# A longer planned slack behind crossbar turns for TensorE's work, in attention followed by a gated feed-forward layer

## The chip, the cores and the metric

The kernel runs on one core of a Trainium2 chip. The metric is the device time of one execution in microseconds (us). A core has five engines that run programs of their own and meet at semaphores: TensorE (PE in the profile, with its weight loads as PEld), VectorE (DVE), ScalarE (ACT), GpSimd (POOL) and SyncE (SP). SP does no arithmetic here; it issues transfers. The kernel before takes 334.26 us, the median of five runs that lie between 333.06 and 335.65 us.

## The reference

Causal attention by blocks of 64 tokens, and then one feed-forward layer whose activation is a swish with a slope of its own for each hidden unit:

```python
# B, H, S, D = 8, 8, 576, 64;  d_model 512, d_ff 2048
scores = scale * np.matmul(q, k.transpose(0, 1, 3, 2))
scores = np.where(block_i >= block_j, scores, -1e9)      # blocks of 64
attn = softmax(scores)
attn_out = np.matmul(attn, v)
x = attn_out.transpose(0, 2, 1, 3).reshape(B * S, H * D)  # 4608 x 512
h = x @ w_in
g = h * (1.0 / (1.0 + np.exp(-beta * h)))
out = g @ w_out
```

## The kernel before

**Two streams of work on one PE.** Attention goes by batch and, within a batch, by pair of heads: a unit `u` is one pair of one batch, four units to a batch, 32 in all. The feed-forward layer goes by chunks of 512 rows of x, nine of them, `r` = 0 to 8. A chunk needs the batches `b0` to `b1` that its rows lie in; for chunks 3 to 7 the last batch is the one with the chunk's own number, and chunk 8 needs no batch beyond 7. The two streams are laid into each other on PE: attention runs about one and a half batches ahead of the chunks that need it.

**Attention.** Q and K have to stand with the head dimension on the partitions. For batches 0 and 1 PE turns them (L634) and DVE copies them out of PSUM. From batch 2 on (`QB = 2`) the turn is a transfer: POOL casts both to bf16 (L665, `QKn`), and SP issues a transfer that turns two units at once through the DMA engines' crossbar into `QKT` (L672, the group of semaphores called `d_T`). There are twelve of these. PE then makes the scores (L708, with the array divided into two halves of 64 rows, the mode `row`): three visits for two units, each an operation of the plan. ACT takes the exponentials into `E` (L724), DVE clears the masked corners (L730, L732), PE multiplies with the values (L764, which bring a column of ones along for the row sums), and DVE divides by the sums (L776, L783) into `xq`.

**From attention to the layer.** The layer needs x turned once more, as `xT`. For batches 0 to 2 PE turns it (L813). From batch 3 on (`XB = 3`) it is again a crossbar transfer from SP, one for each unit (L800, semaphores `d_TX...`), two where the ring buffer of `xT` wraps.

**The layer.** For each chunk there are sixteen up-projections (`fh`, L1000: four matmuls of 128 x 512 into one PSUM bank), each followed by a tanh on ACT (L1010) and a combination on DVE (L1014) that gives sixteen tiles of `gT`. The down-projection (`prod`, L921) is done in chunks 1 to 8 by seven products of half size instead of eight, each in two operations of eight matmuls, with sums of `gT` and of the weights prepared by DVE (L885). So a chunk has 14 such operations of down-projection. In chunk 0 it is the plain one (L1036). Results go out from ACT's queue.

**The order is planned.** No engine's order is written out by hand. `Plan.op` records an operation with an expected duration, a priority (lower goes first), what it depends on and what tiles it needs; `Plan.schedule` then plays the program through, and at each moment gives a free engine the eligible operation of lowest priority. An operation is eligible at its planned `ready` (the planned end of its last dependency, plus `SEM` = 70 ns) plus its own `rest`, and on PE plus `SLACK` = 120 ns:

```python
slack = self.SLACK if e == "PE" else 0.0
if o.ready + o.rest + slack > now + 1e-9:
    heapq.heappush(events, o.ready + o.rest + slack)
    continue
```

The planned end of a transfer is when it has passed its ring plus `LAND` = 2600 ns (L141); its time in the ring is the `xfer` that it was given, 3200 ns for a turn of Q and K and 1100 ns for one of x, if nothing else is in the ring. What comes out of the plan is the order of each engine's instructions, the buffers and banks that tiles are given, and the semaphore waits that follow from them. The planned times themselves are not in the program: on the chip each engine runs its list as fast as the semaphores let it.

`rest` is 0 unless it is set. L827 to L829 set it to 300 ns for operations of PE that depend directly on one of SP or POOL (loads, casts and the turns of Q and K), if they have none yet. This loop stands ahead of the place where the chunks are recorded (L989 on), so the up-projections, which come later, keep 0.

PE's priorities: scores and other work of a unit of batch `b` >= 2 have 994 + 100 * (b - 1.5) + 4.9 * c and a fraction (`pr`), up-projections 1000 + 100 r + j, and the products of the down-projection 1000 + 100 r + 16 for the first two operations, and for the others 103 and up, which is among the next chunk's up-projections. PE also has fillers without use, until 50 us of the plan (L515).

Of the kernel before, what the change touches and what calls it, by code (L numbers as in the profile page):

```python
# [359 lines left out]
def bass_blockwise_causal_attn__then__act_swish_beta_kernel(  # L360
# [10 lines left out]
    with es:  # L371
# [4 lines left out]
        QB, XB, CAST = 2, 3, "POOL"  # L376
# [44 lines left out]
        P = Plan()  # L421
# [6 lines left out]
        def mm(n):  # L428
            return max(n / 2.4 + 3, 55.0)

        def act_t(n, ptr=0):
            return 0.833 * n + 93 + 93 * ptr

        def dve_t(n):
            return (n + 125) / 0.96

        LAG = 1.5
        def pr(u):
            b, c = divmod(u, NPAIR)
            return u if b < 1 else 10 * u if b < 2 else 994 + 100 * (b - LAG) + 4.9 * c  # L440
# [14 lines left out]
        def mk(fn):  # L455
            return lambda g, e: fn(g)
# [13 lines left out]
        for i in range(NQ):  # L470
# [5 lines left out]
            o = P.op("POOL", 200, mk(lambda g, i=i: g.memset(Vn[i][:, 4, :, 64:66], 0.0)), prio=-5)  # L476
# [40 lines left out]
        for i in range(NFILL):  # L517
# [11 lines left out]
            o = P.op("PE", n, ff, deps=[c2, c4], tiles=[tf], lat=n, mode="full", prio=1e6 + i)  # L529
# [6 lines left out]
        for b in range(B):  # L536
# [4 lines left out]
            for h0, h1, e, tt in PARTS[b]:  # L541

                vs = []
                for i in tt:
# [10 lines left out]
                    if e == "SP":  # L555
                        o = P.op("SP", 300 + 550 * n, fv, tiles=[ts], xfer=1400 * n,
                                 prio=3.5 + 0.1 * (h0 > 0) if b == 0 else 4 * b + (3.5 if b < 2 else 0.5),
                                 dma=["d_V", h0, 1])
                    else:
                        o = P.op("POOL", 150 + 1450 * n, fv, tiles=[t], xfer=1400 * n, prio=-30 if b == 0 else 4 * b + (3.5 if b < 2 else 0.5), dma=["d_VP", h0, 1])  # L560
# [9 lines left out]
                for g0 in range(h0, h1, 2):  # L570
                    g1 = g0 + 2

                    def fw(g, e, ts=ts, t=t, g0=g0, g1=g1, n=n):
                        return g.tensor_copy(Vn[t.slot][:, 0:n, g0:g1, 0:64], Vs[ts.slot][:, 0:n, g0:g1, :])  # L574

                    o = P.op("POOL", 60 + 60 * n * (g1 - g0), fw, deps=[*vs, *ones, *vzero], tiles=[ts, t],
                             prio=4 * b + 0.5 - (38.5 - 4.6 * (h0 > 0)) * (b < 1))
# [23 lines left out]
        for u in range(NU):  # L601
# [8 lines left out]
            if b < QB:  # L610

                turned = []
                for w, (nm, src) in enumerate((("Q", q), ("K", k))):
# [7 lines left out]
                    o = ld[nm, u] = P.op("SP", 420, fl, tiles=[ts], xfer=1170, prio=u, dma=["d_S", 0, 1])  # L621
                    o.pkt = 80.0

                    def fn(g, e, ts=ts, tn=tn, p=p, w=w):
# [4 lines left out]
                    o = P.op("POOL" if onp else "DVE", 850 if onp else 750, fn, deps=[o], tiles=[ts, tn],  # L629
                             prio=-40 + 3 * u if onp else -1)  # L630

                    def ft(g, e, tn=tn, pt=pt, p=p, w=w):
                        for i in range(6):
# [4 lines left out]
                    o = P.op("PE", 6 * 43, ft, deps=[o, c4], tiles=[tn, pt, tt_], lat=6 * 43 + 170, mode="full",  # L638
                             prio=pr(u))
# [8 lines left out]
            elif p == 0:  # L648

                for w, (nm, src) in enumerate((("Q", q), ("K", k))):  # L650
                    ts = P.tile("S4")

                    def fl(g, e, ts=ts, src=src, b=b, c=c):
# [3 lines left out]
                    o = P.op("SP", QKI, fl, deps=[o for t in early6 for o in t.users] if b == QB else [],  # L657
                             tiles=[ts], xfer=QKX, prio=u, dma=["d_S4", 0, 1])
# [20 lines left out]
            if b not in JOIN or p == 0:  # L679
# [4 lines left out]
                for grp in visits:  # L684
# [3 lines left out]
                    def fq(g, e, pst=pst, grp=grp, tqk=tqk, b=b):  # L688
                        keep = {}
                        for (uu, g0), ps in zip(grp, pst):  # L690
# [4 lines left out]
                            for t, q0, q1, off in blocks:  # L695
# [18 lines left out]
                    o = P.op("PE", n, fq, deps=cps, tiles=list({id(x): x for x in pst}.values()) + [tqk] + [tes[uu] for uu in sorted({uu for uu, _ in grp})] * (b > 0),  # L714
                             lat=n + 200, mode="row", prio=pr(u) + .2 if len(grp) == 4 else pr(u + 1) + .1 if grp[0][0] > u else
                             pr(u) + .1 + .1 * (grp[0][1] >= 2))
# [3 lines left out]
            for g0 in range(4):  # L720
                o, ps = qk[g0]
# [105 lines left out]
        for o in P.ops:  # L827
            if o.idx > 40 and o.engs == ("PE",) and not o.fill and any(d.engs == ("SP",) or d.engs == ("POOL",) for d in o.deps) and not o.rest:
                o.rest = 300.0  # L829
        win[0].deps += [ld["K", 0]]  # L830
        for o in ld["VP", 0, 4]:
            o.deps += [ld["K", 2]]
# [156 lines left out]
        for r in range(NRC):  # L989
            row = RC * r  # L990
            b0, b1 = row // S, (row + RC - 1) // S
            xd = [xt[4 * b + c] for b in range(b0, b1 + 1) for c in range(4)]
            tg = P.tile("gT")
            gs, hs = [], []
            for j in range(NJ):
                ph, tt = P.tile("P1"), P.tile("th")

                def fh(g, e, ph=ph, j=j, row=row):
                    for c in range(4):
                        z = g.matmul(PS[:, ph.slot, :], w_in[:, c, 128 * j:128 * j + 128], xT[:, c, row % RX:row % RX + RC],  # L1000
                                     start=(c == 0), stop=(c == 3))
                    return z

                o = P.op("PE", 4 * mm(512), fh, deps=xd + [win[j // 4]], tiles=[ph, tg], lat=4 * mm(512) + 170,
                         mode="full", prio=1000 + 100 * r + j)

                hs.append(o)

                def fs(g, e, ph=ph, tt=tt, j=j):
                    return g.activation(th[tt.slot][:], PS[:, ph.slot, :], ACT.Tanh, scale=beta[:, j:j + 1])  # L1010
                a = P.op("ACT", act_t(512, 1), fs, deps=[o, bC], tiles=[ph, tt], lat=act_t(512, 1) + 93, prio=0)

                def fg(g, e, ph=ph, tt=tt, tg=tg, j=j):
                    return g.scalar_tensor_tensor(out=gT[tg.slot][:, j, :], in0=th[tt.slot][:], scalar=1.0,  # L1014
                                                  in1=PS[:, ph.slot, :], op0=ALU.add, op1=ALU.mult)
                gs.append(P.op("DVE", dve_t(512), fg, deps=[a] + (spare.users + spare_x.users if r == 1 else []), tiles=[ph, tt, tg], prio=0))

            for b in range(B):
                if any((S * b + a) // RC - RX // RC == r for a in (0, S - 1 if b < XB else 639)):
                    for c in range(4):  # L1020
                        xt[4 * b + c].deps += hs

            if r in FAST:
                fast(r, row, tg, gs)
                continue

            for w, d0, d1 in [(w, 0, DM) for w in range(4)]:
                po, to = P.tile("P1"), P.tile("ost")


                parts = [(4 * a, 4 * a + 4) for a in range(4)]
                o = None
                for j0, j1 in parts:
                    def fo(g, e, po=po, tg=tg, w=w, j0=j0, j1=j1, d0=d0, d1=d1):
                        for j in range(j0, j1):
                            z = g.matmul(PS[:, po.slot, 0:d1 - d0], gT[tg.slot][:, j, 128 * w:128 * w + 128],  # L1036
                                         w_out[:, j, d0:d1], start=(j == 0), stop=(j == NJ - 1))
                        return z

                    n = (j1 - j0) * mm(d1 - d0)  # L1040
                    was = o
                    o = P.op("PE", n, fo, deps=gs[j0:j1] + wout[j0 // 4:(j1 + 3) // 4],
                             tiles=[po, tg], lat=n + 170, mode="full",
                             prio=1000 + 100 * r + (16 + w + 0.01 * j0 if w == 0 else
                                                     103 + 5.33 * (w - 1) + 1.33 * j0 / 4))
                    o.after = was
                    plain.append(o)

                def fv2(g, e, po=po, to=to, n=d1 - d0):
                    if e == "ACT":  # L1050
                        return g.activation(ost[to.slot][:, 0:n], PS[:, po.slot, 0:n], ACT.Copy, scale=0.5)
                    return g.tensor_scalar(out=ost[to.slot][:, 0:n], in0=PS[:, po.slot, 0:n], scalar1=0.5,
                                           scalar2=None, op0=ALU.mult)
                x = P.op("ACT", act_t(d1 - d0) + 80, fv2, deps=[o], tiles=[po, to], lat=act_t(d1 - d0) + 160, prio=0)

                def fd(g, e, to=to, row=row, w=w, d0=d0, d1=d1):
                    return [g.dma_start(out[row + 128 * w:row + 128 * w + 128, d0:d1], ost[to.slot][:, 0:d1 - d0])]
                P.op("ACT", 500, fd, deps=[x], tiles=[to], xfer=900, dma=["d_ost", to], prio=-1)
# [71 lines left out]
```

## Time and profile before

| | |
|---|---|
| median of five runs | 334.26 us (333.06 to 335.65) |
| the profiled execution | 334.44 us |
| its span, first to last instruction | 332.6 us |
| mean granted TensorE clock | 0.995 |
| up-projections L1000 | 576 weight loads; matmuls 379 ns each |
| down-projections L921 | 896 matmuls, 273 ns each |
| tanh L1010 on ACT | 144, 699 ns each |
| exponentials L724 on ACT | 93 of 1028 ns (and three into `gT`) |
| combination L1014 on DVE | 144, 681 ns each |
| turns of Q and K, L672 | 12, 7.1 us from issue to landing in the median |
| turns of x, L800 | 24, 3.4 us from issue to landing in the median |

Busy time is counted from the start of an instruction to its modelled end, so matmuls that follow each other overlap: the duration of one (379 ns) is more than the distance to the next. How close PE is to its limit is therefore read from distances between starts in a run of equal matmuls, not from durations. The granted clock is at 1.00 in all of the span but a stretch between 23 and 26.5 us and the last few microseconds. The transfers are in PE's way early: the values' arrival ends the longest wait of the first 30 us. Between 60 us and the end PE alternates between scores, values products, up-projections and down-projections, and from 270 us on only the last two are left. The chain of waits that ended last goes through PE for 86% of the span.

### The profile page before, as it was taken

Reading aid. Unit: us, or ns where it says so; the run is one execution under the profiler, and the core shown is the slowest. Engines: PE = TensorE matmul, PEld = TensorE weight load, DVE = VectorE, ACT = ScalarE, POOL = GpSimd, SP = SyncE. Lnnn points to the kernel's source line nnn. Section 1 sums busy time; section 2 is a strip of 40 time slices with the busy share of each in tenths; the row PEclk is TensorE's granted clock in tenths of the full one; section 3 lists DMA queues with packets and bytes.
Section 4 is the critical chain, followed back from the end, with each engine's and each line's share of the span. In section 5 each row is a group of like instructions: output and inputs, shape, how many; then the busy total and the mean of one; then the engine's idle time right before and its main releaser. Section 6 shows DMA issues by size and latency. Waiting matters only on the chain.

```text
span 332.6 us, 7478 instructions
## 1 busy us (share of the span) xinstructions
PE 322.3 (97%) x3112; PEld 205.3 (62%) x3090; DVE 223.3 (67%) x448; ACT 212.5 (64%) x324; POOL 87.6 (26%) x127
## 2 busy tenths in 40 slices
PE   7979999999999999999999999999999999999996
PEld 4666455545576457754665667576566766666685
DVE  4827876588773797357967595668467685666742
ACT  2956984189358886768757857874885555544521
POOL 7646181083182053103630630330000000000000
PEclk9989999999999999999999999999999999999999
DMA  7999999999999879989999999977102210110023
GB/s 211 227 244 211 226 225 204 190 282 212 207 271 211 199 176 194 208 197 199 199 183 210 213 251 198 184 137 124 34 32 41 85 51 34 50 47 32 1 97 126
DMA packets 154993, 53.41 MB, mean 161 GB/s; under 512 B 139072, under 2 KB 154448, under 8 KB 154960
## 3 DMA queue, kind: packets, MB, share of 16 engines
q1 hardware_dynamic: 141200, 40.19, 62.0%
q0 software_dynamic: 5568, 4.36, 8.5%
q10 hardware_dynamic: 8192, 8.39, 7.7%
q8 instruction: 24, 0.39, 0.5%
q14 instruction: 9, 0.07, 0.1%
HBM read 36.71 MB, written 9.44 MB: 139 GB/s over the span
## 4 chain that ended last, share of the span: by engine, by line
PE 86%; ACT 3%; DVE 3%; DMA 2%; SPq 2%; issue 2%; POOL 1%; POOLq 0%
PE PS L1000 35%; PE PS L921 29%; PE PS L764 9%; PE PS L708 7%; PE PS L1036 4%; DMA Vs<-in_v_dram 2%; ACT E L724 2%; PE PS L813 2%; SPq L548 1%; DVE gT L1014 1%; ACT th L1010 1%; PE PS L634 0%; DVE OV L885 0%; SPq L551 0%; DVE ost L945 0%
## 5 line engine op out<-in xcount | busy, mean ns | idle before, releaser
L1010 ACT ACTIVATE th<-PS,beta 128x512 f32<-128x512 f32 x144 | 96.4, 699 | 60.3 <-PE PS L1000 59.6
L1000 PE MATMUL PS<-xT,w_in 128*128 128x512 bf16 x542 | 130.0, 379 | 2.8 <-issue 0.5
L1014 DVE SCALAR_TENSOR_TENSOR gT<-th,PS 128x512 f16<-128x512 f32 x144 | 94.9, 681 | 31.3 <-ACT th L1010 30.7
L724 ACT ACTIVATE E<-PS 128x1024 bf16<-128x1024 f32 x93 | 92.1, 1028 | 27.2 <-PE PS L708 27.1
L1000 PEld LDWEIGHTS PS<-xT,w_in 128*128 128x128 bf16 x576 | 53.3, 98 | 55.6 <-DVE gT L1014 2.2
L921 PE MATMUL PS<-w_out,gT 128*128 128x256 f16 x512 | 63.0, 273 | 0.0
L921 PEld LDWEIGHTS PS<-w_out,gT 128*128 128x128 f16 x512 | 48.9, 98 | 12.2 <-issue 1.5
L574 POOL CAST Vn<-Vs 128x640 bf16<-128x640 f32 (+1 forms) x28 | 22.9, 818 | 94.0 <-DMA Vs<-in_v_dram 92.6
L665 POOL CAST QKn<-ST 128x640 bf16<-128x640 f32 x48 | 38.3, 798 | 27.0 <-DMA ST<-in_k_dram 14.7
L708 PE MATMUL PS<-QKT 64*128 64x320 bf16 (+4 forms) x328 | 36.5, 297 | 0.2 <-ACT E L724 0.2
L764 PEld LDWEIGHTS PS<-Vn,E 128*128 128x128 bf16 x930 | 32.1, 99 | 5.6 <-POOL Vn L574 1.9
L764 PE MATMUL PS<-Vn,E 128*128 128x65 bf16 x930 | 33.1, 196 | 1.7 <-POOL Vn L574 1.7
L942 ACT ACTIVATE ost<-PS 128x512 f32<-128x512 f32 x32 | 19.4, 606 | 21.5 <-PE PS L921 21.5
L921 PE MATMUL PS<-OV 128*128 128x256 f16 x256 | 32.0, 273 | 0.0
L708 PEld LDWEIGHTS PS<-QKT 64*128 64x128 bf16 (+1 forms) x328 | 13.4, 96 | 25.7 <-issue 11.1
L921 PEld LDWEIGHTS PS<-OV 128*128 128x128 f16 x256 | 24.2, 98 | 5.8 <-issue 1.1
L783 DVE TENSOR_TENSOR xq<-PS,inv 128x640 bf16<-128x640 f32 x30 | 24.6, 821 | 0.7
L885 DVE TENSOR_TENSOR OV<-gT 128x1024 f16<-128x1024 f16 x32 | 23.6, 745 | 1.1 <-PE PS L921 0.6
L730 DVE MEMSET E<- 64x64 uint32 x62 | 6.9, 112 | 23.0 <-ACT E L724 21.0
L945 DVE SCALAR_TENSOR_TENSOR ost<-PS,ost 128x512 f32<-128x512 f32 x22 | 15.1, 688 | 7.9 <-PE PS L921 5.5
L921 PE MATMUL PS<-OV,gT 128*128 128x256 f16 x128 | 16.1, 273 | 0.0
L776 DVE RECIPROCAL inv<-PS 128x10 f32<-128x10 f32 x32 | 6.9, 216 | 13.1 <-PE PS L764 12.7
(65 smaller groups left out, 187.1 us busy)
## 6 DMA issues: line engine op xcount, KB each, us to landing
out_dram<-ost ACTq DMA_DIRECT2D x32, 256.0 KB, 3.8
ST<-in_q_dram SPq DMA_DIRECT2D x12, 576.0 KB, 5.4
ST<-in_k_dram SPq DMA_DIRECT2D x12, 576.0 KB, 7.4
Vs<-in_v_dram SPq DMA_DIRECT2D x24, 256.0 KB, 4.0
ST<-in_q_dram SPq DMA_DIRECT2D x8, 288.0 KB, 6.7
ST<-in_k_dram SPq DMA_DIRECT2D x8, 288.0 KB, 6.8
w_in<-in_moe_w_in_dram POOLq DMA_DIRECT2D x4, 512.0 KB, 9.0
w_out<-in_moe_w_out_dram POOLq DMA_DIRECT2D x4, 512.0 KB, 10.1
```

The source lines that it names most:

```text
L574: return g.tensor_copy(Vn[t.slot][:, 0:n, g0:g1, 0:64], Vs[ts.slot][:, 0:n, g0:g1, :])
L665: return g.tensor_copy(QKn[tn.slot][:].rearrange("p a w n -> p (a w n)")[:, 640 * (2 * a + w):][:, 0:640] .rearrange("p (t h d) -> p t h d ...
L708: z = g.matmul(o, QKT[tqk.slot][r, uu % 2, 1, 128 * t + y:128 * t + m + y], x)
L724: return g.activation(E3[es_(te)][:, g0, :, :], PS[:, ps.slot:ps.slot + 2, :], ACT.Exp, scale=0.125)
L764: z = g.matmul(o, eblk(te, t, i, h), Vn[Tv.slot][:, t, 2 * c + h, 0:65], start=(t == 0), stop=(t == i))
L783: return g.tensor_tensor(xq[xq_(tx)][:].rearrange("p i (h d) -> p h i d", h=2), both(pv, 0, 64), x, ALU.mult)
L885: return P.op("DVE", dve_t(SZ * HC / 2), mk(lambda g: g.tensor_tensor(fo(), fx(), fy(), op)), deps=deps, tiles=tiles, prio=prio)
L921: x = g.matmul(PS[:, pw.slot, HM * w:HM * w + HM], fa()[:, j, 128 * w:128 * w + 128], fb()[:, j, :], start=first and (pair or w == 0) and ...
L942: return P.op("ACT", act_t(DM) + 80, lambda g, e: g.activation(ost[to.slot][:], PS[:, ps.slot, :], ACT.Copy, scale=0.5), deps=deps, tiles= ...
L1000: z = g.matmul(PS[:, ph.slot, :], w_in[:, c, 128 * j:128 * j + 128], xT[:, c, row % RX:row % RX + RC], start=(c == 0), stop=(c == 3))
L1010: return g.activation(th[tt.slot][:], PS[:, ph.slot, :], ACT.Tanh, scale=beta[:, j:j + 1])
L1014: return g.scalar_tensor_tensor(out=gT[tg.slot][:, j, :], in0=th[tt.slot][:], scalar=1.0, in1=PS[:, ph.slot, :], op0=ALU.add, op1=ALU.mult)
```

## The change

Two statements are added to what the plan is given. Durations, dependencies, priorities, tiles and the instructions of each operation stay as they are.

```diff
@@ -827,6 +827,9 @@
         for o in P.ops:
             if o.idx > 40 and o.engs == ("PE",) and not o.fill and any(d.engs == ("SP",) or d.engs == ("POOL",) for d in o.deps) and not o.rest:
                 o.rest = 300.0
+        for o in P.ops:
+            if o.engs == ("PE",) and any(d.dma is not None and d.dma[0].startswith(("d_T", "d_TX")) for d in o.deps):
+                o.rest = 1000.0
         win[0].deps += [ld["K", 0]]
         for o in ld["VP", 0, 4]:
             o.deps += [ld["K", 2]]
@@ -1004,6 +1007,7 @@
                 o = P.op("PE", 4 * mm(512), fh, deps=xd + [win[j // 4]], tiles=[ph, tg], lat=4 * mm(512) + 170,
                          mode="full", prio=1000 + 100 * r + j)
 
+                o.rest = 1000.0 if b1 >= XB else 0.0
                 hs.append(o)
```

The first statement finds the operations of PE that were recorded so far and that depend on a turn: the scores of batches 2 to 7, 36 operations. Their `rest` goes from 300 to 1000 ns. The second sets the `rest` of the up-projections of chunks 3 to 8, whose last batch is turned by the crossbar: 96 operations, from 0 to 1000 ns. Both say how late behind a planned landing the plan may put the operation at the earliest; neither adds an instruction or a delay to the program.

## The prediction

> **What bounds the kernel.** I read the engine shares first, then the 40 slices, then a table of busy time by stretch, then TensorE's own waits. From the page:
>
> ```profile
> PE 322.3 (97%) x3112; PEld 205.3 (62%) x3090; DVE 223.3 (67%) x448; ACT 212.5 (64%) x324; POOL 87.6 (26%) x127
> ...
> PE   7979999999999999999999999999999999999996
> ```
>
> The edit cannot act before the first turn of Q and K has landed: it is issued at 51.33 us and lands 12.8 us later, at 64.1. So the stretches after 60 us count, and the waits of PE after 55 us (the waits in full):
>
> ```profile
> 60.00:111.00 51.00, 50.46 (x467) 29.98 (x458) 36.25 (x74) 32.25 (x49) 20.72 (x24) 1.00 1.10 234
> 111.00:270.00 159.00, 157.42 (x1572) 100.44 (x1552) 111.98 (x226) 113.08 (x170) 35.36 (x44) 1.00 0.80 157
> 270.00:316.00 46.00, 45.69 (x297) 29.38 (x302) 31.58 (x49) 25.45 (x38) 0.00 (x0) 1.00 0.08 29
> ```
>
> ```profile
> PE PS L1000 <- issue: 0.5, 3, 0.2
> PE PS L1000 <- DVE gT L1014: 0.3, 2, 0.2
> PE PS L708 <- ACT E L724: 0.2, 1, 0.2
> PE PS L1000 <- DVE OV L885: 0.2, 1, 0.2
> ```
>
> The columns of the first are stretch, length, then busy us of PE, weight loads, DVE, ACT, POOL, then granted clock. From 60 to 316 us PE is busy for 253.57 of 256 us, at full clock. All its waits add to 1.2 us (a matmul record that is missing also shows as idle), and **no wait on a turn is among them**: neither scores (L708) nor up-projections (L1000) ever stand for a DMA. What a longer slack is there to prevent costs nothing in this execution.
>
> Here a rule has to be weighed. The Trainium skill, in Perfetto Trace Analysis, section Identifying the Most-Contended Engine, says that matmul busy time misleads since matmuls overlap, and that the share of the weight loads judges the headroom better. That share is 62%, so by the rule 38% of the span, some 126 us, is open, and a late start could be soaked up. The rows say otherwise: the chain of waits has its last 128 down-projection matmuls (L921) in 13.99 us, 109 ns each, and four of L1000 in 0.86 us, 216 ns each, at the same pitch wherever they run in a row. PE streams without holes, and its weight loads (98 ns) lie beneath. I take the row: soaked up 0, and a microsecond of PE idle is a microsecond of span.
>
> **Part one: the scores.** 36 PE operations read a turned QKT (batches 2 to 7, two pairs each, three visits). Their extra slack goes from 300 to 1000 ns. With the planner's SEM 70 and SLACK 120 they may start 1190 ns behind the planned landing instead of 490. No instruction is added. It moves something only where the planner had put scores less than 1.2 us behind a landing. What the chip shows:
>
> ```profile
> L672 SPq DMA_TRANSPOSE QKT<-QKn x12: 3009/4098/10687, 51.3 to 221.0; - x12
> ...
> DMA to landing us min/median/max: 5.5/7.1/12.8
> ```
>
> From the issues and landings against the first scores of each pair: the pair issued at 167.75 us lands 6.9 later, at 174.6, and is read at 177.03, so 2.4 us of slack, the least of the twelve. The others have 4.6 (139.9 to 144.5), 5.9 (64.1 to 69.95), 6.8 and more, to 20. The scores are held by priority and by free E tiles and banks, not by their turn. The planner's own landing, 3200 + 2600 ns = 5.8 us, is 1.3 us earlier than the median here, so in the plan the slack is rather larger still. I put the moves from this part at 0 to 2 of 12. Cost 0; bounds: below, nothing can be won, as no such wait exists; above, 12 pairs x 0.7 us = 8.4 us if each delay became idle, which needs PE to have nothing else. I take 0, by the wait rows.
>
> A score that does slip by 0.7 us has its exponentials behind it (L724, 1028 ns), then the values product, the normalising, and the xT turn on SP; that turn stands in SP's order ahead of loads of Q, K and V. In the end only chunk 7 would see it: its last xT turn, below.
>
> **Part two: the up-projections.** 96 operations (chunks 3 to 8, 16 each) get 1000 ns where they had 0: earliest start 1190 ns behind the planned landing of xT instead of 190. For 15 of a chunk's 16 that is long past; chunk 8 needs no batch that 7 did not. So five starts count, chunks 3 to 7. Last landing and first weight load of the chunk: 140.3 and 145.0; 168.8 and 171.9; 201.7 and 203.5; 230.2 and 233.4; 267.6 and 268.8. Slack 4.7, 3.1, 1.8, 3.2 and 1.2 us. The timeline around the start of chunk 7 (start, us, engine, line):
>
> ```profile
> 264.98 1.21 SPq L800 DMA_TRANSPOSE xT<-xq  x1
> ...
> 267.15 1.91 PE L921 MATMUL PS<-w_out,gT 128*128 128x256 f16 x16
> ...
> 268.79 3.23 PEld L1000 LDWEIGHTS PS<-xT,w_in 128*128 128x128 bf16 x16
> 268.90 3.40 PE L1000 MATMUL PS<-xT,w_in 128*128 128x512 bf16 x14
> ```
>
> The planner lands an xT turn 1100 + 2600 ns = 3.7 us behind its issue, so at 268.7 here, when the chip had it after 2.6. The chunk's first matmul comes right at that planned moment: **this start is set by the turn, and the edit moves it.** By the same sum chunk 5 (issued 198.1, planned 201.8, started 203.5) may move, chunks 3, 4 and 6 only if the plan runs later than the chip.
>
> What a moved start costs. In 1.0 us PE runs 1.1 products of the chunk before (8 matmuls x 109 ns = 0.875 us each; a chunk has 14, 12.2 us). At 268.8 five of chunk 6's 14 had run (40 matmuls between 264.5 and 268.8), so nine, 7.9 us, are there to cover it. The priorities (1700 + j against 1703 to 1718) then interleave the rest as before, so the order comes together again within chunk 7: end unchanged. At 203.5 and 233.4 products of the chunk before also run on both sides of the start. Only at 145.0 is the cover gone, as chunk 2's last product ends there; but xT landed at 140.3, the PE follows its order and not the planner's clock, so a pause in the plan is none on the chip. If cover failed at all five: 5 x 1.0 = +5.0 us. From below: none of these starts has a wait that could go, so 0.
>
> A product run early is missing later between two up-projections. One of these takes PE 4 x 216 = 864 ns, against 699 ns of ACT and 681 ns of DVE, so a bare pair still leaves ACT 165 ns; with an exponential of 1028 ns in between it doesn't, and the banks must carry that. Nearest row: waits of L1000 on DVE gT, 0.3 us in two. I take 0.2 us in all.
>
> **Part three: mode switches.** Full to row-tiled scores costs 96 ns of pitch (921 to 708, start to start, over the plain 109). All 36 visits of batches 2 to 7 already stand alone between other work, so a new order can't make more, only fewer: 0 to -1 us (ten merged). I take 0.
>
> **The sum**, against the profiled execution: span 332.6, with 334.44 in all, so 1.8 us lies around the span. Scores 0, starts 0, thinned filler +0.2, switches 0: 334.6. The median of the five runs is 0.2 below that execution, so 334.4; I forecast **334.4 us**, no change. A measurement of this kernel tells about 0.5%, 1.7 us, from no change; its five runs lie between 333.06 and 335.65.
>
> **Rivals.**
> - *A hole in front of a chunk, with the clock behind it (slower).* Place: the start of one of chunks 3 to 7, or scores behind a turn, where the new order has no product to run, or a product whose evacuation isn't done. Price, from the only hole of this size in the trace:
>
> ```profile
> 21.76 4.09 PE L764 MATMUL PS<-Vn,E 128*128 128x65 bf16 x90 [1.75 <-POOL Vn L574]
> ...
> 20.00:23.06 3.06, 1.31 (x45) 1.30 (x44) 0.18 (x1) 0.85 (x1) 1.84 (x3) 1.00 1.10 272
> 23.06:26.47 3.41, 3.41 (x60) 3.15 (x57) 1.79 (x6) 1.97 (x10) 3.39 (x5) 0.50 0.86 171
> ```
>
> PE stood for 1.75 us, and 1.3 us after it resumed the clock was 0.50 for 3.41 us, 1.7 us of work lost. The Trainium skill (TensorE: Matmul & The Clock Gate, Part 1) asks for a whole idle window of about 3.4 us before the clock falls; by that a hole that this edit could make is never followed by it, and would cost 1.75 alone (336.2). The row shows a 1.75 us hole with it: 1.75 + 1.7 = 3.4, so 337.8 us. I price by the row. It decides from a hole of about 1 us on, or from several small ones that add to 1.7. For it: 268 us of PE's order may be replanned and every lost piece shows; ACT and DVE are at 71% and 70% between 111 and 270. Against: planned waits are not executed, and fillers are there at four of five starts.
> - *Turns land late in unprofiled runs, and the slack takes those waits away; or visits merge (faster).* The runs spread by 2.6 us and one QKT turn took 12.8 us against 7.1. Against: no such wait in this trace. All that is open after 55 us is 1.2 of waits and 1 of switches: 2.2, so 332.1.
> - *The order hardly differs* (only chunk 7's start moves by one product): 334.3, inside the forecast.
>
> **Chances.** No change 0.58 (of this 0.15 the third rival), slower 0.31, faster 0.11. The range goes from 332.8, half of what could be won and a good set of runs, to 338.0, a hole with its slow clock; about one in ten lies above, for several holes or the +5.0, and one in ten below. The forecast's own range is 333.2 to 335.8.
>
> **What would show it.** Right: the L1000 group starts of chunks 5 and 7 about 1 us, one product, later against their landing; the same starts of the last 128 matmuls within 1 us; PE's waits after 55 us still under 2 us, none on a DMA; PE clock full from 30 us on. Part one wrong: scores of a pair later against their landing by 0.7 us, and other E tiles behind. Wrong in all: a new row of PE waits over 1.7 us in total, or a slice with PEclk under 9 after the first quarter.

## The result, and the profile after

The changed kernel takes 336.46 us in the median of 23 runs (334.45 to 338.53); the kernel before, run beside it, 334.58 us in 42 (332.65 to 337.86). The ratio is **1.0053, with a 95% interval of 1.0033 to 1.0073**: slower by about 1.8 us, a small loss but clear of no change. The profiled execution took 336.35 us, with a span of 334.5.

The change moved less than it seems. Up to the scores of the second pair of batch 2, near 88 us, PE's order is that of before. There the pair's first visit goes one operation of the down-projection later. From there on everything is planned anew.

The stretches and PE's waits after 55 us of the kernel after, in the columns used before:

```profile
60.00:111.00 51.00, 49.37 (x463) 29.80 (x458) 32.20 (x72) 31.11 (x48) 18.30 (x24) 1.00 1.06 218
111.00:270.00 159.00, 156.71 (x1560) 99.30 (x1539) 111.24 (x226) 113.63 (x170) 34.32 (x44) 1.00 0.89 162
270.00:316.00 46.00, 45.69 (x298) 29.52 (x303) 31.90 (x50) 24.89 (x37) 0.00 (x0) 1.00 0.10 35
```

```profile
PE PS L1003 <- issue: 1.6, 6, 0.8
PE PS L708 <- ACT E L724: 1.1, 1, 1.1
PE PS L1003 <- DVE xT L823: 0.2, 1, 0.2
PE PS L924 <- DVE gT L1018: 0.2, 1, 0.2
```

PE loses 1.1 us of busy time between 60 and 111 us and 0.7 between 111 and 270, and nothing after. (L1003 and L924 are before's L1000 and L921.) The waits have grown from 1.2 to 3.1 us, and two single ones make up 1.9 of that.

**The first hole** is ahead of batch 3's first scores. PE's timeline there, first of before, then of after:

```profile
98.69 0.41 PE L708 MATMUL PS<-QKT 64*128 64x512 bf16 x2
...
99.25 1.92 PE L921 MATMUL PS<-w_out,gT 128*128 128x256 f16 x16
101.36 0.39 PE L708 MATMUL PS<-QKT 64*128 64x512 bf16 x2 [0.19 <-ACT E L724]
```

```profile
99.02 0.41 PE L708 MATMUL PS<-QKT 64*128 64x512 bf16 x2
...
99.57 1.05 PE L924 MATMUL PS<-w_out,gT 128*128 128x256 f16 x8
101.68 0.39 PE L708 MATMUL PS<-QKT 64*128 64x512 bf16 x2 [1.06 <-ACT E L724]
```

From the third visit of the pair to batch 3's first scores it takes 2.67 us in the one and 2.66 in the other: the later visit stands for the exponentials of the earlier one, about 1 us each on ACT, and that distance is fixed. Before, two operations of the down-projection (16 matmuls) lie in it; after, one. The other was spent earlier, in the slack of the turn. The hole is that operation's 0.87 us.

**The second hole** is in front of chunk 4 (PE's timeline of after):

```profile
168.97 1.07 PE L764 MATMUL PS<-Vn,E 128*128 128x65 bf16 x30
170.87 1.46 PE L1003 MATMUL PS<-xT,w_in 128*128 128x512 bf16 x6 [0.83 <-issue]
```

The record names nothing ("issue"). Batch 4's last xT turn was issued at 168.21 us and landed at 170.56, as the chunk began (first weight load at 170.62), so the turn is what fits; scores_only, below, names it.

The span is a poor measure of the loss: in the profiled execution of before PE ran at half clock for 3.41 us near 23 us, and in that of after it didn't. So the table below takes the stretch from the first weight load of chunk 1 (63.6 us before, 62.9 after) to the last of chunk 8: 251.7 us before, 253.9 after, 2.2 more. Of these the two holes have 0.87 and 0.8. Distances between matmul starts show that the rest is further waits of at most 0.2 us each, too short for most of them to be listed; what PE does between waits takes as long as before, with 72 changes between full and divided array in either order.

### The profile page after: what moved, and what is told of

Same layout as the page of the kernel before. It is cut to its first block, busy times and chain, and to the rows that moved or that the text cites. A ratio compares the mean times of both kernels' runs of the same rounds, so it can differ in the third digit from the quotient of the medians.

```text
span 334.5 us, 7497 instructions
## 1 busy us (share of the span) xinstructions
PE 321.9 (96%) x3113; PEld 203.8 (61%) x3090; DVE 219.2 (66%) x448; ACT 211.8 (63%) x324; POOL 84.1 (25%) x127
## 4 chain that ended last, share of the span: by engine, by line
PE 80%; DVE 5%; ACT 5%; DMA 3%; issue 3%; SPq 2%; ACTq 0%; POOL 0%
PE PS L1003 32%; PE PS L924 28%; PE PS L708 7%; PE PS L764 7%; PE PS L1040 4%; DVE gT L1018 3%; DMA Vs<-in_v_dram 2%; ACT E L724 2%; SPq L548 2%; PE PS L813 1%; DMA ST<-in_k_dram 1%; DVE xq L783 1%; ACT th L1014 1%; ACT xq L788 1%; ACTq L955 0%
## 5 line engine op out<-in xcount | busy, mean ns | idle before, releaser
L1003 PE MATMUL PS<-xT,w_in 128*128 128x512 bf16 x543 | 130.3, 379 | 3.7 <-issue 1.6
L1003 PEld LDWEIGHTS PS<-xT,w_in 128*128 128x128 bf16 x576 | 53.1, 98 | 57.8 <-issue 2.4
L924 PE MATMUL PS<-w_out,gT 128*128 128x256 f16 x512 | 62.7, 273 | 0.2 <-DVE gT L1018 0.2
L924 PEld LDWEIGHTS PS<-w_out,gT 128*128 128x128 f16 x512 | 49.1, 98 | 11.4 <-DVE gT L1018 0.5
L574 POOL CAST Vn<-Vs 128x640 bf16<-128x640 f32 (+1 forms) x28 | 20.2, 722 | 101.0 <-DMA Vs<-in_v_dram 99.6
L665 POOL CAST QKn<-ST 128x640 bf16<-128x640 f32 x48 | 37.6, 782 | 26.1 <-DMA ST<-in_k_dram 17.2
L708 PE MATMUL PS<-QKT 64*128 64x512 bf16 (+4 forms) x328 | 36.4, 297 | 1.1 <-ACT E L724 1.1
L764 PEld LDWEIGHTS PS<-Vn,E 128*128 128x128 bf16 x930 | 30.9, 97 | 3.8 <-POOL Vn L574 0.5
L764 PE MATMUL PS<-Vn,E 128*128 128x65 bf16 x930 | 31.8, 193 | 0.3 <-POOL Vn L574 0.3
L924 PE MATMUL PS<-OV 128*128 128x256 f16 x256 | 32.0, 273 | 0.0
L924 PEld LDWEIGHTS PS<-OV 128*128 128x128 f16 x256 | 24.2, 98 | 6.4 <-issue 1.1
L732 DVE MEMSET E<- 64x128 uint32 x31 | 5.1, 165 | 17.9 <-ACT E L724 16.7
L1040 PE MATMUL PS<-w_out,gT 128*128 128x512 f16 x64 | 15.7, 380 | 0.0
```

The costliest lines, as they stand in the source:

```text
L665: return g.tensor_copy(QKn[tn.slot][:].rearrange("p a w n -> p (a w n)")[:, 640 * (2 * a + w):][:, 0:640] .rearrange("p (t h d) -> p t h d ...
L708: z = g.matmul(o, QKT[tqk.slot][r, uu % 2, 1, 128 * t + y:128 * t + m + y], x)
L764: z = g.matmul(o, eblk(te, t, i, h), Vn[Tv.slot][:, t, 2 * c + h, 0:65], start=(t == 0), stop=(t == i))
L924: x = g.matmul(PS[:, pw.slot, HM * w:HM * w + HM], fa()[:, j, 128 * w:128 * w + 128], fb()[:, j, :], start=first and (pair or w == 0) and ...
```

## The experiments

Theory A: a product that is spent early is missing ahead of batch 3's first scores. Theory B: the later starts of the chunks are the loss. Theory C: longer slack costs by its length. Later D: the wait for a turn in front of chunk 4 is the rest of the loss, with rival E, that such a hole is taken back later. The stretch and the waits are those of the profiled execution.

The third column was worked out afterwards. The record has the mean granted clock of every run, and for before it is 1.000 (or 0.999) in 83 of them and 0.995 (or 0.994) in 88, with means of 334.2 and 335.4 us; so the mix of the two moves a median by as much as the effects studied here. The column is the difference of the means within these two groups, weighted by the numbers of runs, with the interval from resampling them; the few runs of a lower clock are left out.

| run | ratio to before (95%) | at equal clock, us more (95%) | stretch, us | ahead of batch 3's scores, us | in front of chunk 4, us |
|---|---|---|---|---|---|
| before | 1 | 0 | 251.7 | 0.2 | none |
| after | 1.0053 (1.0033 to 1.0073) | not on record | 253.9 | 1.1 | 0.8 |
| after_again | none | one run | 254.4 | 1.1 | 1.4 |
| scores_only | 1.0055 (1.003 to 1.008) | 1.9 (1.4 to 2.4) | 255.0 | 1.1 | 2.0 |
| ups_only | 0.9991 (0.9967 to 1.0016) | 0.0 (-0.5 to 0.5) | 251.8 | 0.2 | none |
| spend_one | 1.0001 (0.9971 to 1.003) | 0.8 (0.2 to 1.5) | 252.5 | 1.1 | none |
| scores_1500 | 1.003 (1.0009 to 1.0052) | 1.2 (0.8 to 1.6) | 253.6 | none over 0.4 | 1.0 |
| scores_0 | 1.0015 (0.9993 to 1.0036) | 0.8 (0.4 to 1.2) | 252.1 | 0.2 | none |
| turn_first | 1.0044 (1.0019 to 1.0068) | 1.8 (1.4 to 2.2) | 253.5 | 1.1 | none |
| after_fill | 1.005 (1.0028 to 1.0072) | 1.8 (1.4 to 2.1) | 254.3 | 1.1 | 0.2 |
| first_mended | 1.0045 (1.002 to 1.007) | 1.6 (1.0 to 2.2) | 253.2 | 0.2 | none |
| first_mended2 | 1.0018 (1.0 to 1.0037) | 0.5 (0.1 to 0.9) | 252.2 | 0.2 | none |
| both_mended | 1.0045 (1.0018 to 1.0071) | 2.0 (1.5 to 2.7) | 254.1 | 0.2 | none |
| both_mended2 | 1.0028 (1.0005 to 1.0051) | 1.3 (0.8 to 1.8) | 252.7 | 0.2 | none |

### One statement at a time

scores_only has the first statement alone:

```diff
+        for o in P.ops:
+            if o.engs == ("PE",) and any(d.dma is not None and d.dma[0].startswith(("d_T", "d_TX")) for d in o.deps):
+                o.rest = 1000.0
```

> Only the first statement: 1000 ns behind turns for the scores, up-projections back at 0. Theory A (a product of the down-projection is spent ahead of the second pair of batch 2, and is missing ahead of batch 3's first scores): the loss is here. Ratio to before 1.003 to 1.008, and PE stands about 1.1 us for exponentials ahead of batch 3's first scores, where before stood 0.2 to 0.3. Theory B (the later starts of the chunks are the loss): 0.998 to 1.002, and no such hole. Theory C (longer slack costs by its length): between 1.000 and 1.004.

ups_only has the second alone:

```diff
+                o.rest = 1000.0 if b1 >= XB else 0.0
```

> Only the second statement: 1000 ns for the up-projections of chunks 3 to 8, scores back at 300. Theory A: 0.998 to 1.002, PE's waits after 55 us under 1.5 us, and the order of PE like before's up to the start of chunk 7. Theory B: 1.003 to 1.008, with a hole of 0.7 us or more in front of a chunk.

The loss is all in the scores' statement: 1.0055 against 0.9991, as theory A has it. Theory B falls. The second statement does move things, near the start of chunk 5 and from there on, but costs nothing that can be measured. (A forecast missed a detail: PE's order leaves before's at chunk 5, at about 204 us, not at chunk 7.)

Of the scores, one pair matters. The plan gives the same order on every engine for any slack of the scores from 400 to 1000 ns, and the same again if 1000 ns are given to the second pair of batch 2 alone; 200 ns gives the order of before. Of the twelve turns the change thus acts on one, whose first visit before was planned 0.6 us behind the planned landing.

scores_only brought the second hole out larger and with a name. PE's and SP's timelines there:

```profile
172.42 1.07 PE L764 MATMUL PS<-Vn,E 128*128 128x65 bf16 x30
175.46 1.24 PE L1000 MATMUL PS<-xT,w_in 128*128 128x512 bf16 x5 [1.97 <-DMA xT<-xq]
```

```profile
165.27 4.31 SPq L672 DMA_TRANSPOSE QKT<-QKn  x1
169.63 2.57 SPq L800 DMA_TRANSPOSE xT<-xq  x2
```

Here the new plan has put the QKT turn of batch 5's first pair ahead of the last xT turn of batch 4 on SP. Before, they went the other way round (164.58 and 167.75). PE stands for a turn, in a kernel that was given a longer slack behind turns, and in before it nowhere does.

### The first hole by itself

spend_one is the kernel before with one operation of PE's finished order moved; nothing is planned anew:

```diff
         P.schedule()
+        L = P.order["PE"]
+        a = next(i for i, o in enumerate(L) if o.mode == "row" and abs(o.prio - 1058.8) < 1e-6)
+        m = L.pop(a + 1)
+        m.start = L[a - 1].start - 0.01
+        L.insert(a - 1, m)
```

> The kernel before, and in PE's finished order one operation of the down-projection (8 matmuls, 0.875 us) put ahead of the third scores visit of batch 2's second pair instead of behind it. Nothing is planned anew. Theory A: the wait for exponentials ahead of batch 3's first scores grows from 0.2 to 0.3 to about 1.1 us; the time grows by 0.3 to 0.9 us, ratio 1.001 to 1.003. If the hole comes from the other moves that a new plan brings: the wait stays at 0.2 to 0.3 us and the ratio at 1.000.

The hole is made to order (PE's timeline of spend_one):

```profile
101.07 0.41 PE L708 MATMUL PS<-QKT 64*128 64x512 bf16 x2
...
101.63 1.05 PE L921 MATMUL PS<-w_out,gT 128*128 128x256 f16 x8
103.74 0.39 PE L708 MATMUL PS<-QKT 64*128 64x512 bf16 x2 [1.06 <-ACT E L724]
```

In the trace it stays to the end of chunk 8: a stretch of 252.5 us, 0.8 more than before. The ratio by itself, 1.0001, misses theory A's forecast of 1.001 to 1.003, with an interval that holds both 0 and 0.3%: 11 of spend_one's 14 runs had the full clock, but little more than half of before's (35 of 63). At equal clock it is 0.8 us slower (0.2 to 1.5), as in the trace. So one operation that runs earlier is a loss by itself, though not the whole of it.

### The length of the slack

scores_1500 sets 1500 ns instead of 1000 in scores_only:

```diff
-                o.rest = 1000.0
+                o.rest = 1500.0
```

> The first statement with 1500 ns instead of 1000, no second statement; this moves the first pair of batch 2 as well. Theory C (longer slack costs by its length): more than scores_only, 1.006 to 1.012. Theory A (what counts is how many products are left between two visits that wait for the same exponentials): no relation to the length; 0.998 to 1.004, whichever way the products fall, and with two products between the third visit of batch 2's second pair and batch 3's first no hole over 0.4 us there.

1.003 is not more than 1.0055, where theory C asked for 1.006 or more. The hole ahead of batch 3's first scores isn't there, with the two operations back in their place; others are, on a turn of x in front of chunk 4 (1.0 us), and on exponentials in front of chunk 2 (0.8):

```profile
PE PS L1000 <- DMA xT<-xq: 1.0, 1, 1.0
PE PS L1000 <- ACT E L736: 0.8, 1, 0.8
```

scores_0 takes the slack of the scores away:

```diff
+        for o in P.ops:
+            if o.engs == ("PE",) and any(d.dma is not None and d.dma[0].startswith(("d_T", "d_TX")) for d in o.deps):
+                o.rest = 0.0
```

> The scores' slack behind turns taken from 300 ns to 0; up-projections as before. My first reading (no wait of PE on a turn, so the slack protects nothing): 0.997 to 1.003 and no wait of the scores on a turn over 0.3 us. Rival (turns land later than planned and the slack hides it): a wait of the scores on a turn of 0.5 us or more, ratio above 1.003.

No wait of the scores on a turn: the 300 ns of before protect against none here either. (The new order that comes of it isn't free: at equal clock it is 0.8 us slower, of which the stretch shows 0.4.) All of PE's waits after 55 us, with turns of Q and K that took from 5.0 to 12.1 us to land:

```profile
PE PS L1000 <- DVE gT L1014: 0.6, 4, 0.2
PE PS L708 <- ACT E L724: 0.3, 2, 0.2
PE PS L1000 <- issue: 0.2, 1, 0.2
```

### The second hole

turn_first is scores_only with the two turns exchanged in SP's finished order:

```diff
         P.schedule()
+        Q = P.order["SP"]
+        a = max(i for i, o in enumerate(Q) if o.start < 169000 and o.dma[0].startswith("d_TX"))
+        Q[a - 1].start = Q[a].start + 0.01
+        Q[a - 1], Q[a] = Q[a], Q[a - 1]
```

> The program of scores_only with one change in SP's finished order: the last xT turn of batch 4 is issued ahead of the QKT turn of batch 5's first pair, as in the kernel before, not behind it. PE's order is that of scores_only. Theory D (the second half of the loss is chunk 4's start standing for that turn): the 2.0 us wait in front of chunk 4 falls under 0.5 us, the 1.1 us wait ahead of batch 3's first scores stays, ratio to before 1.001 to 1.004. Rival E (a hole there is taken back later, since other work then comes earlier): the wait falls and the ratio stays at 1.004 to 1.007.

after_fill is the changed kernel with one down-projection operation put ahead of chunk 4:

```diff
         P.schedule()
+        L = P.order["PE"]
+        a = next(i for i, o in enumerate(L) if o.mode == "full" and o.prio == 1400)
+        b = next(i for i in range(a, len(L)) if 1300 < L[i].prio % 10000 < 1330 or 1403 <= L[i].prio < 1418 and L[i].tiles[0].cls == "P1" and L[i].prio != int(L[i].prio))
+        m = L.pop(b)
+        m.start = L[a].start - 0.01
+        L.insert(a, m)
```

Here `b` is the next down-projection operation behind the chunk's first two up-projections.

> The changed kernel, and in PE's finished order one operation of the down-projection (0.875 us) put from behind chunk 4's first two up-projections to ahead of them. Theory D: the wait of 0.8 us in front of chunk 4 goes, the rest stays, ratio to before 1.002 to 1.004 against 1.0053 of the changed kernel. Rival E: 1.005 to 1.006, with the 0.8 us showing up again in a later wait of PE.

> The changed kernel once more, for another profiled execution. If the holes belong to the order: 1.0 to 1.2 us ahead of batch 3's first scores and 0.4 to 2 us in front of chunk 4 again. If the one in front of chunk 4 was an accident of one execution, it is missing here.

The hole in front of chunk 4 is no accident: 0.8 and 1.4 us in two executions of the changed kernel. In turn_first it is gone, and the stretch falls from 255.0 to 253.5 us, by three quarters of the hole. The ratio, 1.0044 against 1.0055, lies between what theory D and rival E ask for, and doesn't tell them apart. In after_fill the filler covered most of the hole, and PE then stood elsewhere, by the record for turns, so the stretch stayed at 254.3:

```profile
PE PS L764 <- DMA xT<-xq: 0.5, 1, 0.5
PE PS L708 <- DMA QKT<-QKn: 0.4, 1, 0.4
```

For a hole that is filled rather than removed, rival E is right: what is late is still late.

### Putting the first place back

first_mended is the changed kernel, and both_mended is turn_first, each with the operations from the second pair of batch 2 to batch 3's first scores put into before's order on PE, ACT and DVE:

```diff
         P.schedule()
+        for e, i, w in [('PE', 183, [748, 1230, 1164, 1232, 749, 1233, 1237, 1238, 758, 1241, 1242, 761, 750, 1243, 1244, 782, 770, 1247, 1248]), ('ACT', 82, [751, 753, 1231, 1165, 1166, 755, 757, 767, 769, 1239, 1240, 763, 765, 1245]), ('DVE', 128, [752, 1221, 754, 1222, 1234, 756, 1235, 768, 1236, 759, 760, 762, 764, 766, 1246, 786])]:
+            by = {o.idx: o for o in P.order[e][i:i + len(w)]}
+            P.order[e][i:i + len(w)] = [by[x] for x in w]
...
+        for o in P.ops:
+            o.start = o.rank
```

> The program of scores_only with both places put back by hand in the finished order: the operations of PE, ACT and DVE from the second pair of batch 2 to batch 3's first scores in the order of the kernel before, and the last xT turn of batch 4 ahead of the QKT turn as in turn_first. All that follows keeps the order of scores_only. If the two holes are the loss: waits of 0.2 to 0.3 us ahead of batch 3's first scores and under 0.5 us in front of chunk 4, ratio to before 0.998 to 1.002. If the rest of the new order costs too: the same small waits and 1.003 or more, with other waits of PE that add to 1 us.

> The changed kernel with the first place alone put back by hand: the operations of PE, ACT and DVE from the second pair of batch 2 to batch 3's first scores in the order of the kernel before. If the product spent early costs in time what the trace shows (0.9 us): the wait there is 0.2 to 0.3 us and the ratio to before is 1.001 to 1.004 against 1.0053. If the time is taken back later: the wait goes and the ratio stays at 1.005 to 1.006, with a longer wait in front of chunk 4.

Neither gave the time back (1.0045 both), and the profile says why: the wait has gone one step on. PE's waits of first_mended:

```profile
PE PS L764 <- ACT E L724: 1.1, 1, 1.1
PE PS L1000 <- issue: 0.8, 5, 0.2
```

(both_mended also stood 0.6 us for a turn of x, in front of chunk 5.) In before's order the values product (L764) follows batch 3's first scores at once. But the banks are those of the new plan, and the ones that it was given are freed by batch 3's first exponentials. An order that is copied without its banks is another order. The corrected pair leaves that product where the new plan has it, behind two operations of the down-projection:

> As both_mended, but put back only up to batch 3's first scores: there the values product went ahead of two down-projection operations and stood 1.1 us for exponentials, since the banks it was given in the new plan are those that batch 3's first exponentials free. Now the two operations run in between, as in scores_only. If the two holes are the loss: no wait over 0.5 us from 90 to 110 us and in front of chunk 4, ratio to before 0.998 to 1.002. If the rest of the new order costs too: 1.003 or more.

> As first_mended, with the same correction. If the product spent early costs in time what the trace shows (0.9 us): no wait over 0.5 us from 90 to 110 us, the wait in front of chunk 4 stays, ratio to before 1.001 to 1.004. If it is taken back later: 1.005 to 1.006 and a longer wait in front of chunk 4.

first_mended2 has one listed wait of 0.2 us left after 55 us, and **1.0018 (1.0 to 1.0037) where the changed kernel has 1.0053**; its stretch is 252.2 us:

```profile
PE PS L708 <- ACT E L724: 0.2, 1, 0.2
```

(Its profile and both_mended2's have all 576 matmuls of the up-projections. The others lack 33 to 35 of them, and each wait of 0.2 us on "issue" there can be such a missing record; the stretches don't depend on this.) PE's order behind that place is the changed kernel's. So most of the loss hangs on this place; the intervals 1.0 to 1.0037 and 1.0033 to 1.0073 barely meet. The wait in front of chunk 4 went with it, which I had not expected: PE, the last turn of batch 4 and the chunk all came earlier. Why the turn gained more than the chunk, one execution doesn't tell, and I leave it open. both_mended2, at 1.0028 with an interval of 1.0005 to 1.0051, missed its band of 0.998 to 1.002. With both holes gone PE's listed waits after 55 us are down to 0.4 us in all, but the stretch, 252.7 us, is still 1.0 more than before's, and so is the time at equal clock (1.3 us, 0.8 to 1.8). A third of it is in one place, a late up-projection of chunk 4:

```profile
193.75 1.07 PE L764 MATMUL PS<-Vn,E 128*128 128x65 bf16 x30
195.00 1.04 PE L1000 MATMUL PS<-xT,w_in 128*128 128x512 bf16 x4 [0.19 <-DVE gT L1014]
```

The two start 1.25 us apart, where 0.90 is usual (108.46 to 109.36 us in before), so PE lost 0.35 us to a combination on DVE. The list shows 0.19 of it, as idle time counts from the modelled end of a matmul. The rest is in pieces of 0.13 us and less, scattered over the new order. So the first place is the largest part of the loss, and the order that follows from it costs something too.

No version beat the kernel before. ups_only (0.9991) can't be told from it; scores_0 (1.0015) can't by its ratio, and is slower at equal clock.

## Why the prediction was right and wrong

The range (332.8 to 338.0 us) held the 336.46, but the likeliest case was no change at 334.4, and the loss is real, at 0.5% with an interval of 0.3% to 0.7%.

- **No wait on a turn in before, so nothing to win.** Right: the slack could be taken away altogether (scores_0) and no wait on a turn of Q and K came up.
- **A microsecond of PE idle is a microsecond of span** (the row, against the share of the weight loads). It held in the trace: 0.9 us of hole gave 0.8 us of stretch in spend_one. With the weight loads at 62% nothing soaked it up.
- **Part one, scores: 0 to 2 of 12 moved, cost 0.** The count was right, one pair. The cost was the step that failed. I read the slack from the chip (6.8 us for this pair) and argued that the plan's was larger still; the plan had 0.6, since it had the turn ready at 87.7 us where the chip had it at 82.1. The 3200 + 2600 ns that I used hold for an empty ring; in the plan other transfers were in it, and this turn took 9.3 us from issue to landing. And I priced a moved operation by whether PE had something to do at that moment, which it had. The price falls due later: at the next place where the distance is fixed by ACT.
- **Thinned filler, +0.2 us.** This is the term that was mis-sized. The mechanism stood in the text (a product run early is missing later), placed between up-projections and priced by waits of 0.3 us in two. It came between two scores visits, and cost 0.87 us, a whole operation.
- **"In the end only chunk 7 would see it."** Wrong: chunk 4 did, with 0.8 and 1.4 us, which fits a turn of x.
- **Part two, up-projections, 0.** Right (ups_only, 0.9991). The starts of chunks 5 and 7 were expected to move: the order does change from chunk 5 on, and chunk 7 begins 3.1 us behind its landing there instead of 1.2.
- **Mode switches, 0.** Right: each still costs 96 ns of pitch, and there are as many as before (72 in the stretch).
- **The rival of a hole with the clock behind it.** Half right. There were holes, at both kinds of place that it named (scores of a turned pair, though it was exponentials that they stood for, and the start of a chunk). The slow clock didn't follow: the 2.0 us wait of scores_only in front of chunk 4 was answered with full clock, so that the holes cost their length and the 3.4 us was too much. I had priced by the one row that I had, against the rule of the Trainium skill (TensorE: Matmul & The Clock Gate, Part 1) that asks for an idle window of about 3.4 us; for this hole the rule was the better guide. The place differs: the row was from the start of the kernel, as the last section shows.
- **Late turns in unprofiled runs, faster.** No run shows it.
- **The signs.** The clock stayed full from 30 us on, as named for right. The waits after 55 us came to 3.1 us, where the prediction asked for under 2.

## What to carry to other kernels

Where an engine's order is planned, a slack is not a delay but a swap: something else runs in it, and it is missing where it would have run. Before pricing such a change, look for the next place behind it where the distance between two operations is fixed by another engine (here two score visits and the exponentials, 2.67 us), and count what is left to fill it. And read a slack against the plan's own times: what the trace shows between a landing and its use tells whether a wait can occur, not whether the planner will move something.

The plan can also be played through for both versions before anything runs. Its own end goes from 337.0 us to 338.3 with the change (338.5 with the first statement alone, 337.2 with the second alone). That was a warning of about the right size, and I didn't use it. It is no more than a warning: for scores_1500 and scores_0 the plan ends within 0.1 us of before, and both came out slower at equal clock.

## What the runs showed of the hardware that was not expected

PE's half clock near the start comes and goes with the same program. Of the fourteen profiled executions here, five (before, spend_one, scores_1500, turn_first, first_mended) have one stretch of 3.41 us at 0.50 between 23 and 34.5 us, the others none, and PE's order is the same in all up to 60 us. (The profiles of after and ups_only have no row of granted clock; there it is the pitch of the matmuls, 216 ns for 512 columns, that tells.) In these five a wait of PE ended 0.3 to 2.0 us ahead of the stretch: 1.75 us in before, 1.23, 1.79, 1.16 and 1.10 in the others. In eight of the nine without it, PE's longest wait between 20 and 30 us was 0.83 us or less; both_mended had one of 1.10 and kept its full clock. So early in the kernel the stretch goes with waits of more than a microsecond, shorter than the window of the rule above, but the length alone doesn't decide. Later it doesn't hold at all: the 2.0 us wait of scores_only at 175 us, amid dense matmuls, left the row of granted clock full throughout:

```profile
PEclk9999999999999999999999999999999999999999
```

A stretch of 3.41 us at half clock is 1.7 us of work lost, and the runs of before with a mean clock of 0.995 are 1.3 us slower than those with 1.000. That is as much as the changes studied here, and it hides them unless runs of equal clock, or the stretch behind it, are compared.
